# An RWKV-5 and mixture-of-experts kernel: the loads of an item's r and k, and of its keys and values, cut in two

## The chip, the cores and the metric

The kernel runs on one core of one Trainium2 chip. The metric is the device time of one execution in microseconds (us). The kernel before took 382.85 us, the median of three runs (382.5 to 382.89).

## The reference, cut to what matters

An attention block of the RWKV-5 kind is followed by a mixture of experts that routes each token to one expert. Batch B = 4, heads H = 8, sequence S = 768, head dimension 48; all values are float32.

```python
for t in range(S):                                   # attention, for each batch and head
    cur = einsum('bhd,bhe->bhde', u * k[t], v[t])
    y[t] = einsum('bhd,bhde->bhe', r[t], state + cur)
    state = w * state + einsum('bhd,bhe->bhde', k[t], v[t])
x = y as (B, S, 384)
for b, s:                                            # mixture of experts
    fresh = argmax(x[b, s] @ w_gate)                 # 8 experts
    e = fresh, or the token's before it where sigmoid(x[b, s] @ w_local) >= 0.5
    out[b, s] = softmax(x[b, s] @ w_gate)[e] * (relu(x[b, s] @ w1[e]) @ w2[e])   # 384 -> 1024 -> 384
```

## The kernel before, in words

The attention is computed in 16 items. An item is one batch and one pair of heads (`n` from 0 to 15, `b, hp = divmod(n, 4)`), with the sequence cut into NCH = 6 chunks of 128 tokens. For an item TensorE computes the scores of a chunk against itself (`scores`, L288), the part of a token's own key (`own`, L267), the keys times values that a chunk adds to the state (`added`, L248), and the outputs from inside the chunk (`inside`, L297) and from the states before it (`before`, L310). VectorE masks the scores (L290), multiplies by v (L273), scans over the states (L254) and divides the keys by the decay (`keys`, L236). GpSimd prepares three products for each item (`scale`): `pd`, r times k (L216); `rw`, r times the decay (L229, for the first three items on VectorE); `ke`, the keys of the states times the decay (L212). ScalarE copies the outputs from PSUM (L318, and L331 after they are turned), and when a batch of four items is done it stores the batch with one transfer to memory, `x_d` (L334).

An item's input comes by `load(n)`, called three items ahead in `run`. Three DRAM arrays are read, each with 128 partition rows for an item:

- `rk`, 768 KB: a row has the 768 values of r and then the 768 values of k, 6144 bytes. Four tiles take turns (`AHEAD` = 4).
- `kv`, 584 KB: a row has the 576 values of the keys (`VB` = 576) and then the 592 of the values with their padding, 4672 bytes. Five tiles take turns. `ke` (L212) reads the keys and `added` and `inside` read the values.
- `vT`, 384 KB: v turned, 3072 bytes in a row, read by L273. Four tiles take turns.

All these transfers are issued by SyncE (SP), which does nothing else here and issues in the order of the program. It waits before each transfer until the tile that it overwrites is free. It also waits for one of eight semaphores: the builder puts the transfers of SP and ScalarE into one order and gives them the eight in turn, so each waits until the transfer eight places before it in that order has landed. The same holds for ScalarE's `x_d`: the wait stands in ScalarE's own queue, and the copies of later items stand behind it.

Item 0 is a case of its own: its `rk` already comes by two transfers, one for chunks 0 to 2 and one for chunks 3 to 5.

The order of the work on each engine is the order in which `run` calls the steps; no scheduler reorders it. After the 16 items the experts follow: ten blocks of tokens (`Experts.run`), with a block's weights `w1t` and `w2t` loaded by SP and ScalarE, tokens gathered from `x_d` and results scattered to the output by GpSimd.

Of the kernel before, what the change touches and what calls it, by code (L numbers as in the profile page):

```python
# [21 lines left out]
B, H, S, DH = 4, 8, 768, 48  # L22
# [30 lines left out]
VB = NCH * 2 * DH  # L53
# [8 lines left out]
class Attention:  # L62
# [126 lines left out]
    def load(self, n):  # L189
        nc = self.nc  # L190
        b, hp = divmod(n, HP)
        rk, vT, kv = self.rks[n % AHEAD], self.vTs[n % AHEAD], self.kvs[n % (AHEAD + 1)]
        if n:
            nc.sync.dma_start(out=rk.rearrange("p a c t -> p (a c t)"), in_=self.rk_d[b, hp])
        else:
            for z in (slice(0, C2), slice(C2, NCH)):
                nc.sync.dma_start(out=rk[:, :, z], in_=self.rk_d[b, hp].rearrange("p (a c t) -> p a c t", a=2, c=NCH)[:, :, z])
        nc.sync.dma_start(out=kv, in_=self.kv_d[b, hp])
        nc.sync.dma_start(out=vT.rearrange("p a c t -> p (a c t)"), in_=self.vT_d[b, hp])
        self.items[n].update(b=b, hp=hp, rT=rk[:, 0], kT=rk[:, 1], vT=vT,  # L200
                             k=kv[:, :VB].rearrange("p (c x) -> p c x", c=NCH), v=kv[:, VB:])
# [1549 lines left out]
```

## Time and profile before

| | before |
|---|---|
| median of three runs | 382.85 us (382.5 to 382.89) |
| the profiled execution | 382.2 us |
| its span, first to last instruction | 380.4 us |
| TensorE clock granted, share of full | 0.997 |
| PE busy | 366.9 us, 96% |
| DVE busy | 248.7 us, 65% |
| POOL busy | 151.3 us, 40% |
| ACT busy | 107.1 us, 28% |
| DMA | 17765 packets, 74.97 MB |
| rk, time from issue to landing | 5.7 / 9.0 / 12.2 us (least, median, most) |
| kv, time from issue to landing | 6.1 / 7.7 / 12.6 us |

The profile is of one execution. The page gives busy times of each engine, 40 slices of the span (9.5 us each), the DMA queues and the costliest groups of instructions. PE is TensorE's matmuls and PEld its weight loads. A busy PE isn't PE at its peak, since the ends of pipelined matmuls are modelled. A line that ends in `[1.51 <-DMA kv<-in_kv_dram]` says that the engine was idle for 1.51 us and that the landing of that transfer ended the idle time. `ACTq` and `SPq` are the sequencers, which issue transfers while the engine itself is idle.

The loads of the items run from 0.8 to about 85 us, the attention to about 110 us.

### The profile page before, as it was taken

What the parts mean: (1) busy time and instruction counts of PE and PEld (TensorE: products, weight loads), DVE (VectorE), ACT (ScalarE), POOL (GpSimd) and SP (SyncE); (2) the same over time, 40 slices, a digit from 0 to 9 for tenths busy, and PEclk for the clock granted to TensorE, in tenths of its full rate; (3) what the DMA queues carried; (4) which work ended last, traced back from release to release, by engine and by line L of the source; (5) the groups of instructions that cost most, each with busy time, mean ns of one, the idle gap of its engine ahead of it and who ended that gap; (6) DMA issues with size and microseconds to landing.
All of it is one profiled execution on the core that took longest, in us unless ns stands there. A gap on an engine that the chain in (4) does not pass through costs nothing. (4 is left out here: it accounts for less than half of the span.)

```text
span 380.4 us, 9693 instructions
## 1 busy us (share of the span) xinstructions
PE 366.9 (96%) x3846; PEld 323.9 (85%) x3846; DVE 248.7 (65%) x720; ACT 107.1 (28%) x295; POOL 151.3 (40%) x213
## 2 busy tenths in 40 slices
PE   8999999999999999999999999999999999999992
PEld 7776777776769989999999999999898899899971
DVE  6888778887853736587557857758658758466400
ACT  4132233232322112223323233233233233232210
POOL 8789999886222043211423213223323123012022
PEclk9999999999999999999999999999999999999998
DMA  7999999973648872811561254146146156063011
GB/s 254 412 411 407 408 398 310 372 307 126 210 157 301 318 274 68 317 60 40 200 219 41 72 209 179 38 173 227 57 167 229 37 179 229 12 225 161 3 37 36
DMA packets 17765, 74.97 MB, mean 197 GB/s; under 512 B 2761, under 2 KB 6618, under 8 KB 15408
## 3 DMA queue, kind: packets, MB, share of 16 engines
q1 hardware_dynamic: 10336, 56.89, 40.1%
q0 software_dynamic: 3424, 9.52, 7.6%
q10 hardware_dynamic: 3952, 7.87, 5.7%
q8 instruction: 32, 0.52, 0.6%
q14 instruction: 21, 0.17, 0.1%
HBM read 64.83 MB, written 9.51 MB: 195 GB/s over the span
## 5 line engine op out<-in xcount | busy, mean ns | idle before, releaser
L1308 POOL DMA_INDIRECT out_dram<-yo,sid x27 | 26.6, 987 | 102.4 <-ACT yo L1303 79.0
L1159 PE MATMUL h<-exT,w1t 128*128 128x168 f32 (+4 forms) x240 | 54.9, 327 | 0.0
L1163 DVE TENSOR_TENSOR hT<-h,hs 128x168 f32<-128x168 f32 (+3 forms) x60 | 21.1, 351 | 46.3 <-PE h L1159 30.5
L1082 POOL DMA_INDIRECT xg<-x_d,gid x29 | 31.1, 1074 | 35.7 <-DVE sm L905 17.4
L1159 PEld LDWEIGHTS h<-exT,w1t 128*128 128x128 f32 x240 | 41.7, 190 | 0.3 <-issue 0.3
L1109 PE MATMUL h<-exT,w1t 128*128 128x192 f32 (+1 forms) x192 | 38.3, 338 | 0.0
L1228 PE MATMUL y<-factors,sums 128*128 128x192 f32 x168 | 36.8, 326 | 0.0
L1159 PE MATMUL h<-xs,ws 128*128 128x168 f32 (+4 forms) x144 | 35.2, 326 | 0.0
L216 POOL TENSOR_TENSOR pd<-rk 128x384 f32<-128x384 f32 x32 | 31.4, 1002 | 8.6 <-PE y L267 6.2
L290 DVE TENSOR_TENSOR am<-pair,kept 128x768 f32<-128x768 f32 x32 | 30.0, 951 | 7.1 <-PE pair L288 6.9
L1109 PEld LDWEIGHTS h<-exT,w1t 128*128 128x128 f32 x192 | 32.3, 190 | 1.5 <-issue 0.2
L1159 PEld LDWEIGHTS h<-xs,ws 128*128 128x128 f32 x144 | 25.5, 190 | 4.3 <-ACT hs L1166 1.2
L1228 PEld LDWEIGHTS y<-factors,sums 128*128 128x128 f32 x168 | 28.9, 190 | 0.0
L212 POOL TENSOR_TENSOR ke<-kv,endT 128x288 f32<-128x288 f32 x32 | 24.9, 799 | 1.8 <-DMA kv<-in_kv_dram 1.8
L288 PE MATMUL pair<-rw,kw 48*64 48x128 f32 (+1 forms) x768 | 23.5, 249 | 1.3 <-DVE lt L349 0.4
L297 PE MATMUL y<-am,kv 128*64 128x128 f32 x360 | 23.9, 276 | 0.8 <-DVE y L273 0.8
L229 POOL TENSOR_TENSOR rw<-rk,tab 128x384 f32<-128x384 f32 x26 | 23.6, 929 | 0.2 <-DMA rk<-in_rk_dram 0.2
L1228 PE MATMUL y<-w2t,hT 128*128 128x192 f32 x96 | 23.0, 328 | 0.0
L1096 DVE COPY exT<-tp 128x384 f32<-128x384 f32 (+6 forms) x29 | 14.0, 489 | 13.7 <-PE tp L1095 13.5
L288 PEld LDWEIGHTS pair<-rw,kw 48*64 48x64 f32 x768 | 19.6, 133 | 3.8 <-issue 2.1
L297 PEld LDWEIGHTS y<-am,kv 128*64 128x64 f32 x360 | 20.0, 137 | 2.4 <-DVE y L273 1.0
L318 ACT COPY xT<-y 128x768 f32<-128x768 f32 x15 | 12.0, 799 | 34.0 <-PE y L310 34.0
(301 smaller groups left out, 737.9 us busy)
## 6 DMA issues: line engine op xcount, KB each, us to landing
w1t<-in_w_dram SPq DMA_DIRECT2D x8, 1536.0 KB, 6.7
w2t<-in_w_dram SPq DMA_DIRECT2D x8, 1536.0 KB, 7.2
rk<-in_rk_dram SPq DMA_DIRECT2D x15, 768.0 KB, 9.0
kv<-in_kv_dram SPq DMA_DIRECT2D x16, 584.0 KB, 7.7
vT<-in_vT_dram SPq DMA_DIRECT2D x16, 384.0 KB, 8.3
x_d<-x ACTq DMA_DIRECT2D x4, 1152.0 KB, 4.6
w1t<-in_w_dram SPq DMA_DIRECT2D x2, 768.0 KB
w2t<-in_w_dram SPq DMA_DIRECT2D x2, 768.0 KB, 4.5
```

The lines of the kernel that those rows point to most:

```text
L212: nc.gpsimd.tensor_mul(t["ke"][:, p::2], t["k"][:, p::2], spread(self.endT[:, p, hp], 1, C2))
L216: nc.gpsimd.tensor_mul(t["pd"][:, z], t["rT"][:, z], t["kT"][:, z])
L229: engine.tensor_mul(t["rw"][:, z], t["rT"][:, z], spread(pw, 1, z.stop - z.start))
L288: nc.tensor.matmul(sc[f * DP:(f + 1) * DP, h, i, x:], lhsT=t["kw"][q, c, o * DP:(o + 1) * DP], rhs=t["rw"][q, c, x:], start=True, stop=True)
L290: return lambda: nc.vector.tensor_mul(t["am"][:, g], sc, spread(self.kept[:, g:g + 3], 1, 2))
L297: nc.tensor.matmul(t["y"][h][p * DP:(p + 1) * DP, c2 * P:(c2 + 1) * P], lhsT=t["v"][:, (2 * c + h) * DH:(2 * c + h) * DH + DP], rhs=t["am" ...
L1082: self.nc.gpsimd.indirect_dma_start(out=xg[:n], out_offset=None, in_=self.x_d[:rows], in_offset=bass.IndirectOffsetOnAxis(ap=u["gid"][:n, ...
L1109: nc.tensor.matmul(h[:, :n], lhsT=u["w1"][:, m, kk, :], rhs=u["xT"][:, kk, :], start=(kk == 0), stop=(kk == DK - 1))
L1159: nc.tensor.matmul(out, lhsT=a, rhs=b, start=start and k == 0, stop=stop and k == len(terms) - 1, skip_group_check=True)
L1163: nc.vector.tensor_tensor(out, a, b, op=Alu.add)
L1228: return lambda: nc.tensor.matmul(bank[:, x * half:(x + 1) * half], lhsT=a, rhs=b, start=(j == 0 and x == 0), stop=(j == FK // 2 - 1), ski ...
L1308: self.nc.gpsimd.indirect_dma_start(out=out.rearrange("n (h d) -> (n h) d", h=2) if half else out, out_offset=bass.IndirectOffsetOnAxis(ap ...
```

## The change

`load` issues `rk` (for items 1 to 15) and `kv` (for all items) as two transfers instead of one. The r half and the k half of `rk` have rows of 3072 bytes; the keys' half of `kv` has rows of 2304 bytes and the values' half of 2368. The same bytes go to the same places of the same tiles. Who waits for a tile now waits for the half that it reads. `vT`, item 0's `rk` and everything else in the source stay.

```diff
         if n:
-            nc.sync.dma_start(out=rk.rearrange("p a c t -> p (a c t)"), in_=self.rk_d[b, hp])
+            for a in range(2):
+                nc.sync.dma_start(out=rk[:, a].rearrange("p c t -> p (c t)"), in_=self.rk_d[b, hp][:, a * S:(a + 1) * S])
         else:
             for z in (slice(0, C2), slice(C2, NCH)):
                 nc.sync.dma_start(out=rk[:, :, z], in_=self.rk_d[b, hp].rearrange("p (a c t) -> p a c t", a=2, c=NCH)[:, :, z])
-        nc.sync.dma_start(out=kv, in_=self.kv_d[b, hp])
+        for z in (slice(0, VB), slice(VB, None)):
+            nc.sync.dma_start(out=kv[:, z], in_=self.kv_d[b, hp][:, z])
         nc.sync.dma_start(out=vT.rearrange("p a c t -> p (a c t)"), in_=self.vT_d[b, hp])
```

## The prediction

> **What bounds the kernel now.** I read the page first, for where PE is full and where the transfers are.
>
> ```profile
> span 380.4 us, 9693 instructions
> ...
> PE   8999999999999999999999999999999999999992
> ...
> POOL 8789999886222043211423213223323123012022
> ...
> DMA  7999999973648872811561254146146156063011
> GB/s 254 412 411 407 408 398 310 372 307 126 210 157 301 318 274 68 317 60 40 200 219 41 72 209 179 38 173 227 57 167 229 37 179 229 12 225 161 3 37 36
> ```
>
> A digit is a tenth of a slice of 9.5 us. PE is full from the second slice to the end. The transfers are full only in the slices up to about 60 us, at some 410 GB/s, while the items' inputs come in. The chain that ended last says nothing here (it breaks off after 1 us, at the last scatter), so I asked the list of waits for the first 110 us, where all of the change lies.
>
> ```profile
> POOL pd L216 <- DMA rk<-in_rk_dram: 2.4, 2, 1.3
> ...
> POOL ke L212 <- DMA kv<-in_kv_dram: 1.8, 2, 1.5
> ...
> PEld mp L248 <- POOL ke L212: 1.2, 2, 0.6
> ```
>
> The columns are us in total, times, and longest. GpSimd is the only engine that waits for these loads, 4.4 us with one wait of 0.2 for rw, all in the first 28 us. TensorE never waits for one. The list for PE alone has 1.5 us of GpSimd, for the identity at the start, and after that only VectorE (0.9, 0.8, 0.5, 0.4) and small rests. The 1.2 us above is of weight loads (PEld), which run ahead of the matmuls; PE itself had no gap there. So the question is how far GpSimd is ahead of PE when it waits. The timelines of the two, GpSimd first:
>
> ```profile
> 11.15 1.96 POOL L216 TENSOR_TENSOR pd<-rk 128x384 f32<-128x384 f32 x2 [1.04 <-DMA rk<-in_rk_dram]
> ...
> 27.50 1.55 POOL L212 TENSOR_TENSOR ke<-kv,endT 128x288 f32<-128x288 f32 x2 [1.51 <-DMA kv<-in_kv_dram]
> ```
>
> ```profile
> 15.45 0.90 PE L267 MATMUL y<-pd,w_t 48*64 48x384 f32 x8
> ...
> 30.24 0.65 PE L248 MATMUL mp<-kv,ke 128*48 128x48 f32 x20
> ```
>
> Item 1's pd ends at 13.1 and is used at 15.45. Item 4's ke ends at 29.05 and is used at 30.24, behind PE's own work without a gap. The margins are 2.3 and 1.2 us, and the second is the smallest I find. Items 2 and 3 have 3 us or more. Followed back from 47 us, PE's order goes through VectorE, one ScalarE copy and itself, and reaches no transfer and no GpSimd work but the identity at 1.5 us. From 44 us on PE has next to no gap, so whatever delays it before that arrives whole at the end.
>
> The last view is ScalarE's timeline around the first store of x_d, and PE's after it.
>
> ```profile
> 40.77 0.40 ACTq L334 DMA_DIRECT2D x_d<-x  x1
> 43.82 0.80 ACT L318 COPY xT<-y 128x768 f32<-128x768 f32 x1 [3.09 <-PE y L310]
> ```
>
> ```profile
> 44.68 0.88 PE L267 MATMUL y<-pd,w_t 48*64 48x384 f32 x8
> ```
>
> The copy ends at 44.62 and frees the only buffer of y; PE's L267 starts at 44.68. This copy is on the path that sets the end, and the store of x_d stands ahead of it in ScalarE's queue.
>
> **What the Trainium skill says.** The page "DMA: Bandwidth & Descriptors" has three sections that bear on this. "Why small descriptors are slow (HBM only)" puts a fixed cost on each packet. The trace agrees: its packets on SP's queue take 234 ns (median) with 6144 bytes, 180 with 4672, 121 with 3072 and 65 with 1536, which is a line of 0.0366 ns a byte plus 9 ns. "Why a DMA increments its semaphore by 16 and not by 1" says that a transfer has landed only when all its engines have counted. The trace agrees: item 8's rk counts first at 40.40 and last at 43.12. "Queues, rings and completion order" says that an engine takes its rows in turn, a packet at a time. The store of x_d, landing 13.4 us after its issue amid a full SP queue, fits that.
>
> **The change part by part.**
>
> *Packets.* A transfer of 128 rows gives each of 16 engines 8 packets and one count of 9 ns. One rk was 8 x 234 + 9 and becomes 2 x (8 x 121 + 9): 73 ns more. One kv was 8 x 180 + 9; halves of 2304 and 2368 bytes are 93.3 and 95.7 ns on the line: 8 x 9 + 9, some 80 ns more. An item had 4.31 us of packets and gets 4.46. That is 0.15 us more an item (3.5%). Up to item 8 it adds 1.2 us to a landing, over all 16 items 2.4 us. It is hidden: item 1's rk lands at 11.23 instead of 11.08 and pd ends at 13.3, used at 15.45. Later items land ahead of use, rk 5 to 11 (issued 18.65 to 52.68, landed 30.21, 34.49, 38.77, 43.12, 48.23, 54.40, 58.66; first used by rw at 32.85 to 64.18) by 2.6 to 5.5 us, more than the 0.75 to 1.7 us added. Without that cover it would be up to 2.4 us.
>
> *Issue.* 31 more transfers at 0.33 us each (up to 0.6 at the start) are 10 us or so on SP over 80 us. SP waits there anyway: 26.9 us for VectorE's y alone. Nothing computes on SP.
>
> *Finer waits.* rw needs only r, kw only k, ke only the keys. Item 4's keys land 0.1 to 0.9 us earlier (half a kv is 0.73 us at 410 GB/s, less 0.64 us of extra packets, and the slowest engine's lag falls on one half or the other). GpSimd's wait of 1.51 us becomes 0.6 to 1.4. pd needs both halves, so its two waits grow by 0.15 and 0.3 us. PE takes nothing of it, by the margins above: worth 0. GpSimd gets an extra semaphore wait for many pd, at 17 to 51 ns for such an instruction, 16 of them under 0.8 us, on an engine that is ahead.
>
> *Eight semaphores in turn.* Eight transfers were 2.7 items and are now 1.6, some 2.8 MB, 6.9 us of work at 410 GB/s. A load in this stage lands 10 to 12 us after its issue because it queues; now about 7. The engines don't run dry: the slowest lags the fastest by up to 2.7 us, and a piece of weights issued onto idle engines counts after 3.6 us of which 1.9 are its own packets. That leaves 6.9 - 0.9 - 2.7 = 3.3 us of work against 1.7 of delay. Cost 0.
>
> *The store of x_d.* This is the part that can show. By the listing of the changed program the first store (0.40 us on ScalarE) now takes the semaphore of **item 8's r half**; before it was that of item 6's vT, landed at 36.88, long before 40.77. When does the r half land? Before, item 8's rk landed at 43.12. Add 1.2 us of packets and take off the k half, 8 x 121 + 9 = 0.98: 43.34. The store then ends at about 43.8, and L318 behind it was to start at 43.82. Behind L318 waits L267 and all of PE. So the central cost is 0 with no margin: each 0.1 us of lateness costs 0.1 us. The trace has no such halves with a stride of twice their length, so I bound it. From below, with the packets' overhead overlapped, the half lands at 42.2 and costs 0; a gain through it is excluded, since the copy waits for PE anyway. From above, the mean of vT's packets while the loads run is 132 ns instead of 121; with 2 x 132 against a mean of 249, and the same on kv, the overhead is some 0.26 us an item, 2.1 us by item 8, and the half lands at 44.2, costing 0.85 us. I take 0.15 us. The other three stores find their semaphores free: by the listing they follow loads of items 11, 14 and 15, landed at about 60, 79 and 84 us against stores at 64.64, 90.25 and 114.89. The first store's later landing (about 53 us) holds up item 11's r, which has 5.5 us to spare.
>
> *Sum.* 0 + 0 + 0 + 0.15. The profiled execution would go from 382.2 to about 382.35 (span 380.4 to 380.55). It lay 0.65 us under the median of the runs; on the median it is 382.85 + 0.15 = 383.0 us.
>
> **The rivals.**
>
> *The store stops ScalarE.* Slower, by one mechanism: item 8's r half lands later than about 43.35 us, L334 waits for it, L318 behind it, L267 behind that. For it: no margin in the sum. Against: the landing comes out just at the limit. At the upper bound it costs 0.85 us, 383.7 us; a further instruction-fetch packet on the slowest engine (16 KB, 1.0 us median in this trace) makes it 384.6. It counts as slower from a landing at about 44.1.
>
> *GpSimd's waits were on the path.* For it: 4.4 us of waits for these loads, and GpSimd full from 28 to 67 us. If half a kv were saved there and PE followed, 0.7 to 1.4 us: 381.5 to 382.1 us. Against: margins of 1.2 us and more, and GpSimd waits for PE at 69, 81 and 94 us.
>
> *The loads pace the stage.* Then the 0.15 us an item count, 16 x 0.15 = 2.4 us: 385.2 us. Against: PE has no wait for a load, and the loads end at 85 us, the items at 110.
>
> *The change does nothing at all.* 382.85 us; it can't be told from my forecast.
>
> **How the numbers follow.** Forecast (with no effect) 0.58, 382.5 to 383.5 around 383.0. ScalarE stopped by more than the bound 0.23, GpSimd's waits on the path 0.14, loads as the pace 0.05. A measurement of this kernel can't tell 0.2%, 0.77 us, from no change. Faster than 382.08: most of the third case, 0.12. Slower than 383.62: the second and fourth, 0.28. Same: 0.60, the forecast with what is small of the others. The range has the forecast, the second up to its 0.85 us and somewhat over, and the weak end of the third: 382.1 to 384.1.
>
> **What would show it.** Right: rk and kv land 7 us after issue; SP's packets grow by 31 x 144 = 4464; an item's loads pace at 4.46 us; GpSimd's wait for kv shrinks and those for rk grow a little, with PE's times up to 43 us within 0.1; L334's first store at 43.3 to 43.4 instead of 40.77. Wrong: L318 of item 4 starts later than 43.9 (second case), PE reaches 43 us earlier (third), or PE or PEld wait for a load (fourth).

## The result, and the profile after

| | before | after |
|---|---|---|
| median, on one chip | 382.6 us (381.78 to 385.73) | 383.45 us (382.29 to 387.21) |
| the profiled execution | 382.2 us | 382.74 us |
| its span | 380.4 us | 381.0 us |
| packets of SP's queue | 10336 | 14800 |
| rk, median from issue to landing | 9.0 us | 6.7 us |
| kv, the same | 7.7 us | 7.2 us (keys), 6.3 us (values) |

The ratio is 1.0031, with a 95% interval of 1.0015 to 1.0046; the medians themselves differ by 0.85 us. A second comparison, on chip 3, gave 1.0044 (1.0028 to 1.0061), and 1.54 us between the medians. By the ratios the change makes the kernel about 0.3 to 0.4% slower, 1.2 to 1.7 us. Here and below the medians are of all executions, and the ratios leave out those more than 1.5% above the fastest of their kernel, which matters for `odd_even`, `merged`, `by_partitions` and `used_rows`.

From the page of the changed kernel, the rows that answer to those shown of before:

```profile
span 381.0 us, 9728 instructions
...
PE   7999999999999999999999999999999999999992
...
DMA  7999999993657871820661254146146156064011
GB/s 256 400 397 397 396 391 350 361 319 131 192 175 272 326 293 52 313 79 22 218 215 45 62 207 186 43 173 221 63 167 227 39 179 229 10 225 163 3 37 36
```

The second to sixth slice carried 412 to 398 GB/s before and carry 400 to 391 now. That is 3% less, what the packets' fixed cost takes. The engines are as full as before (row DMA), so the backlog of loads lasts longer.

The waits of the first 110 us in the changed kernel (us in total, times, longest):

```profile
POOL pd L218 <- DMA rk<-in_rk_dram: 2.3, 2, 1.6
PEld mp L250 <- POOL ke L214: 1.8, 3, 0.6
...
POOL ke L214 <- DMA kv<-in_kv_dram: 0.6, 1, 0.6
```

GpSimd's wait for kv went from 1.8 to 0.6 us and that for rk from 2.4 to 2.3. In the list of PE's own waits still no line names a transfer. GpSimd's timeline shows the same two instructions as before, and then PE's:

```profile
11.23 1.96 POOL L218 TENSOR_TENSOR pd<-rk 128x384 f32<-128x384 f32 x2 [0.67 <-DMA rk<-in_rk_dram]
...
26.34 1.56 POOL L214 TENSOR_TENSOR ke<-kv,endT 128x288 f32<-128x288 f32 x2 [0.56 <-DMA kv<-in_kv_dram]
```

```profile
15.91 0.90 PE L269 MATMUL y<-pd,w_t 48*64 48x384 f32 x8
...
30.70 0.66 PE L250 MATMUL mp<-kv,ke 128*48 128x48 f32 x20
```

Item 4's `ke` starts at 26.34 instead of 27.50, but PE uses it at 30.70 instead of 30.24. GpSimd gained over a microsecond and PE took none of it. PE's 0.46 us of delay in this execution come from its start: `w_t`, a transfer that the change doesn't touch, landed at 3.26 us instead of 2.81. In most other kernels below it landed at 2.76 to 2.83, so this delay is of one execution. ScalarE around the first store, and PE after it:

```profile
42.61 0.40 ACTq L336 DMA_DIRECT2D x_d<-x  x1
44.23 0.80 ACT L320 COPY xT<-y 128x768 f32<-128x768 f32 x1 [3.23 <-PE y L312]
```

```profile
45.08 0.88 PE L269 MATMUL y<-pd,w_t 48*64 48x384 f32 x8
```

The store did wait for item 8's r half, which landed at 42.53. But it was issued 1.6 us before the copy behind it could start, and the copy waited for PE alone.

So where is the time? I compared the start of each PE matmul with the same matmul of the kernel before. In a second profiled execution of the change (`after_again`, span 381.7) PE is 0.33 us ahead at 45 us, 1.14 us behind at 66 us, and 1.30 us behind at the end of the program. The loss arises between 46 and 66 us. PE's timeline there shows it, first before and then `after_again`:

```profile
51.80 0.71 PE L248 MATMUL mp<-kv,ke 128*48 128x48 f32 x20
57.09 0.66 PE L248 MATMUL mp<-kv,ke 128*48 128x48 f32 x20
```

```profile
51.47 0.29 PE L250 MATMUL mp<-kv,ke 128*48 128x48 f32 x3
52.16 0.57 PE L250 MATMUL mp<-kv,ke 128*48 128x48 f32 x17 [0.40 <-issue]
...
57.31 0.29 PE L250 MATMUL mp<-kv,ke 128*48 128x48 f32 x4
57.98 0.56 PE L250 MATMUL mp<-kv,ke 128*48 128x48 f32 x16 [0.38 <-issue]
```

Twenty matmuls of one kind, with the same inputs, break off after the third or fourth. "issue" means that PE waited for nothing that the profile shows. These two breaks cost 0.55 and 0.54 us, and a third at 63.4 us 0.38. That is the whole 1.47 us. The first profiled execution, the one of the table above, shows less of it: PE ends 0.63 us behind, of which `w_t` accounts for 0.45, and of these three breaks it has only the first, with 0.27 us. How many breaks there are differs from one execution to the next.

The breaks stand at fixed places of PE's program. Counted from its start these are among matmuls 725, 852, 978, 1105, 1231, and on in steps of 126 or 127. The table of queues has a row for such a rhythm:

```profile
q8 instruction: 32, 0.52, 0.5%
```

These are 32 packets of 16 KB with PE's instructions, about 1 us each. The Trainium skill, "Runtime: NRT & Kernel Launch", section "Instruction fetch mechanics", says that a sequencer fetches its program through a DMA queue of its own in blocks of 16 KiB, which are 256 instructions. The trace agrees on the size: 127 matmuls with a weight load each are 254. I call such a block a page, and its first matmul its boundary. The same section calls the crossing of a block mostly hidden. Here it isn't. From the packets' times in the traces, for the pages that begin at five of these matmuls: how long after the previous page's boundary the fetch started, how long after the fetch's end PE ran the page's first matmul (both us), and the largest distance between the starts of two matmuls there (ns; about 100 at most where nothing stops PE there).

```
matmul          725              852              978              1105             1231
before        3.78 1.46 392   3.70 1.44 323   2.99 1.38  73   1.11 2.39  38   1.61 2.46   7
after         3.97 1.51 538   3.70 1.44 328   3.14 1.52 330   1.68 2.22  39   2.19 1.89   7
after_again   3.79 1.39 264   3.73 1.40 326   3.56 1.33 606   3.35 1.41 585   3.14 1.35 316
extra_packets 3.70 1.49 265   3.58 1.56 327   3.67 1.52 880   3.33 1.42 600   3.32 1.09 316
fewer_bytes   3.89 1.55 540   1.12 3.21  74   2.31 2.02  73   2.64 1.69  38   0.60 3.65   7
```

(The last two kernels are explained below.) PE never runs a page sooner than 1.09 us after its fetch has ended. Where its distance is 230 ns or more, that lag is always 1.1 to 1.6 us; this holds over the pages from 725 to 1991 in all the traces, apart from matmul 1864, where PE waits for VectorE, and from `by_partitions`, where PE waits for data too. With the engines full of loads the fetch starts 3.0 to 4.0 us after the boundary; with room on them, often at 1 to 2 us. In the first case a page takes 3.7 + 1.0 + 1.45 = 6.2 us. PE runs a page in 5.3 us or so here (before, 51.94 to 57.22). So PE is paced by its own instructions while the load queue is full. Before, that held for pages 725 and 852 and just not for 978. (Outside the table it also held for pages 600 and 1612, with distances of 363 and 452 ns, 1.43 and 1.45 us after a fetch's end.) After, of the pages from 978 to 1231 one stops PE in `after` and all three in `after_again`. I call this the fetch theory. The 0.33 us by which `after_again` leads at 45 us have the same source: pages 600 and 725 stopped it 0.19 and 0.13 us less than before.

### The profile page after: what moved, and what is told of

Same layout as the page of the kernel before. It is cut to its first block, busy times and chain, and to the rows that moved or that the text cites. A ratio compares the mean times of both kernels' runs of the same rounds, so it can differ in the third digit from the quotient of the medians.

```text
span 381.0 us, 9728 instructions
## 1 busy us (share of the span) xinstructions
PE 367.0 (96%) x3846; PEld 323.8 (85%) x3846; DVE 248.2 (65%) x720; ACT 107.1 (28%) x295; POOL 151.2 (40%) x213
## 3 DMA queue, kind: packets, MB, share of 16 engines
q1 hardware_dynamic: 14800, 56.89, 40.6%
## 5 line engine op out<-in xcount | busy, mean ns | idle before, releaser
L299 PE MATMUL y<-am,kv 128*64 128x128 f32 x360 | 23.9, 276 | 0.8 <-DVE y L275 0.8
L299 PEld LDWEIGHTS y<-am,kv 128*64 128x64 f32 x360 | 20.0, 137 | 2.4 <-DVE y L275 1.0
```

The costliest lines, as they stand in the source:

```text
L299: nc.tensor.matmul(t["y"][h][p * DP:(p + 1) * DP, c2 * P:(c2 + 1) * P], lhsT=t["v"][:, (2 * c + h) * DH:(2 * c + h) * DH + DP], rhs=t["am" ...
```

## The experiments

Each ratio is to the kernel before on the same chip, with a 95% interval. Differences are to the changed kernel where nothing else is said.

### The change again, each half of it, and the store moved

These four were compared together, before the fetch theory was formed. The change itself:

> The changed kernel once more, beside the others on one chip, as their yardstick. The store theory (ScalarE's first store of x_d waits for item 8's r half, and the copy L320 behind it starts late when that half lands after about 43.8 us) and the packet theory (0.15 us more of packets an item delays work somewhere) both expect +0.2 to +0.3% against the kernel before; the store theory also expects single runs that scatter upward by 1 us and more. If the difference was an accident of the first measurement, it is within 0.1%.

Measured: 383.95 us, ratio 1.0044 (1.0028 to 1.0061). Its trace is the one shown above.

`rk_only` cuts rk and leaves kv whole; `kv_only` the reverse.

```diff
 rk_only
-        for z in (slice(0, VB), slice(VB, None)):
-            nc.sync.dma_start(out=kv[:, z], in_=self.kv_d[b, hp][:, z])
+        nc.sync.dma_start(out=kv, in_=self.kv_d[b, hp])
 kv_only
-            for a in range(2):
-                nc.sync.dma_start(out=rk[:, a].rearrange("p c t -> p (c t)"), in_=self.rk_d[b, hp][:, a * S:(a + 1) * S])
+            nc.sync.dma_start(out=rk.rearrange("p a c t -> p (a c t)"), in_=self.rk_d[b, hp])
```

> Only rk by two transfers. The first store's semaphore is then that of item 7's kv, expected to land at about 40.8 us, well before the copy behind it is due. The store theory expects no loss: within 0.1% of the kernel before. The packet theory expects about half: +0.1 to +0.15%.

> Only kv by two transfers. The first store's semaphore is that of the values' half of item 7, expected to land at about 40.9 us, before the copy behind it is due. The store theory expects no loss: within 0.1%. The packet theory expects about half: +0.1 to +0.15%. If finer waits for the keys help GpSimd and through it PE, this one is faster than before.

Measured: `rk_only` 382.89 us, ratio 1.0015 (1.0001 to 1.0029); `kv_only` 382.78 us, ratio 1.0012 (1.0003 to 1.0021). Each half costs something, and together they come to 1.0027, within the interval of the whole. No single half, and no wait for a single half, is the cause. It is something that adds up.

`late_store` issues the store of `x_d` behind the copy that stood behind it (`turn` keeps the tile in `self.unsent`, and `store()` sends it after `before`).

```diff
 turn
-            nc.scalar.dma_start(out=self.x_d[...], in_=x)
+            self.unsent = b, x
 run
             self.before(n - 1)
+            self.store()
```

> The changed kernel with the stores of x_d moved in ScalarE's order behind the copy L320 of the same round, so that their wait for a semaphore has nothing urgent behind it. The store theory expects the loss to go: within 0.1% of the kernel before. The packet theory expects it to stay: +0.2 to +0.3%. In the profile L320 of item 4 starts within 0.05 us of PE's end in both cases.

Measured: 383.6 us, ratio 1.0038 (1.0026 to 1.005). ScalarE in `late_store`, the store now behind the copy:

```profile
43.52 0.80 ACT L321 COPY xT<-y 128x768 f32<-128x768 f32 x1 [3.02 <-PE y L313]
43.72 0.40 ACTq L344 DMA_DIRECT2D x_d<-x  x1
```

The store can stop nothing there, and the loss stays. The store theory falls.

### Packet time without a cut: `extra_packets`

The kernel before, and one small transfer more an item.

```diff
+        self.extra = once.tile([P, 8, 64], F32, name="extra")
 load (of the kernel before, rk and kv whole)
         nc.sync.dma_start(out=vT.rearrange("p a c t -> p (a c t)"), in_=self.vT_d[b, hp])
+        nc.sync.dma_start(out=self.extra[:, n % 8], in_=self.rk_d[b, hp][:, :64])
```

> The kernel before, with rk, kv and vT whole, and after each vT one more transfer of 128 rows of 256 bytes into a tile that nobody reads: 8 x (9 + 9.4) + 9 = 156 ns of packets an item, about what the change adds (153), without cutting anything. Packet and fetch theory: as slow as the change, ratio 1.0015 to 1.0045, GB/s of the stretch 3% lower on data (some 400), PE's gaps at its instruction pages in more places than before. Rival, the cut of rk and kv itself (finer waits, five transfers an item): 0.9995 to 1.001.

Measured: 383.56 us against 381.77, ratio 1.0045 (1.003 to 1.006). The packets of 256 bytes took 18 ns each. PE at the same two places:

```profile
51.40 0.29 PE L250 MATMUL mp<-kv,ke 128*48 128x48 f32 x3
52.36 0.57 PE L250 MATMUL mp<-kv,ke 128*48 128x48 f32 x17 [0.67 <-issue]
...
57.52 0.29 PE L250 MATMUL mp<-kv,ke 128*48 128x48 f32 x4
58.21 0.56 PE L250 MATMUL mp<-kv,ke 128*48 128x48 f32 x16 [0.39 <-issue]
```

The change's loss is there with no load cut: the same packet time, the same places, the same size. The rival that the cut itself costs (finer waits, five transfers an item) expected at most 1.001, and falls. It does add a fourth transfer to an item's three, so the number of transfers could still be what costs. The two runs above speak against that. `rk_only` and `kv_only` also have four transfers an item (item 0's `rk` apart) and as many packets more as this kernel, but they add 73 and 80 ns of packet time an item instead of 156, and they cost 0.15 and 0.12% instead of 0.45%. The intervals don't meet (at most 1.0029 against at least 1.003), though they were taken on two chips. The loss follows the packets' time and not their number.

This trace, the slowest of the kernel's seven executions, also lost 1.66 us at a later page (matmul 1612, fetch 5.64 us after the boundary), and the break had a second cost. Two matmuls lie 2.11 us apart there; from 84.62 us on the granted clock was 0.50 for 3.41 us, and in that stretch PE lost another 1.45 us. The traces of before, `after` and `after_again` have no such stretch between 7 and 377 us, so it is no part of the loss shown above. The whole loss at the end of this trace is thus more than its median shows.

### The loads made shorter: `fewer_bytes`

```diff
-        nc.sync.dma_start(out=vT.rearrange("p a c t -> p (a c t)"), in_=self.vT_d[b, hp])
+        if n not in range(4, 11):
+            nc.sync.dma_start(out=vT.rearrange("p a c t -> p (a c t)"), in_=self.vT_d[b, hp])
```

> The change, but vT of items 4 to 10 isn't loaded, so their y is multiplied by an older item's v: this leaves out 2.75 MB of loads and no computation. Every half of rk and kv is as in the change. Fetch theory: with 1.0 us less of packets an item the engines aren't full from about 45 us on, instruction fetches start 1 to 2 us after the page before instead of 3 to 4, PE's gaps at 52, 58 and 63 us go, ratio 0.996 to 1.0005. Rivals in which the halves themselves cost (their waits on GpSimd, number of transfers, the store of x_d): the loss of the change stays, 1.003 to 1.0045.

The total, 2767.3 us, answers nothing: with other values of x the routing went to the program's general path for the experts, which is another program. The attention ran as in the change, and its PE timeline can be read:

```profile
51.44 0.66 PE L251 MATMUL mp<-kv,ke 128*48 128x48 f32 x20
56.73 0.66 PE L251 MATMUL mp<-kv,ke 128*48 128x48 f32 x20
```

Both breaks are gone, as the table's last row says, though every half of rk and kv is loaded as in the change. At matmul 1612 PE is 0.80 us ahead of the kernel before (79.00 against 79.80), where `after_again` is 1.1 us behind (80.92). The expectation in the ratio stays untested; that on the places was met, and the fetches of pages 852 to 1231 started 0.6 to 2.6 us after the boundary where 1 to 2 were expected.

### The pages moved in PE's program: `shifted`

```diff
-        self.align(26)
+        self.align(0)
```

> The change without the 26 small matmuls of `align` at the start (they compute nothing that is used). PE's program is 26 matmuls shorter ahead of the attention, so that the pages in which PE's instructions come (126 to 127 matmuls each) end 26 matmuls later in the program. Fetch theory: the gaps of PE without a releaser near 40, 52 and 58 us leave L250 (at its 3rd to 5th matmul of 20) and turn up 26 matmuls later, in L299 after its 8th to 10th matmul of 24, whichever of these pages is late in this execution; they stand again 1.3 to 1.5 us after the end of the page's fetch. Rival, something that L250 itself waits for and the trace doesn't show (ke, the buffer mp): the gaps stay at L250. Time: 1.001 to 1.006 of before, since the fetches come as late as before.

The 26 calls are 52 matmuls in the trace (3846 before, 3794 here), so the places had to move by 52, not 26. Counted from the fourth matmul of L250, 52 further are 17 of L250, 24 of L299 and 11 of L312. PE in `shifted`:

```profile
47.41 0.65 PE L250 MATMUL mp<-kv,ke 128*48 128x48 f32 x20
...
49.36 0.68 PE L312 MATMUL y<-rw,S 48*48 48x128 f32 x11
50.28 0.56 PE L312 MATMUL y<-rw,S 48*48 48x128 f32 x9 [0.25 <-issue]
...
55.22 0.68 PE L312 MATMUL y<-rw,S 48*48 48x128 f32 x11
56.08 0.48 PE L312 MATMUL y<-rw,S 48*48 48x128 f32 x9 [0.18 <-issue]
...
60.96 0.68 PE L312 MATMUL y<-rw,S 48*48 48x128 f32 x12
63.01 0.48 PE L312 MATMUL y<-rw,S 48*48 48x128 f32 x8 [1.37 <-issue]
```

The breaks left L250, which runs whole, and stand in L312 after its 11th or 12th matmul, 1.40, 1.32 and 1.40 us after the end of a fetch. Against `after_again`, matmul by matmul, PE gains 0.26, 0.32, 0.60 and 0.55 us at the four old places and loses 0.51, 0.45 and 1.55 at the three new ones shown. Nothing that L250 waits for is the cause; the page is. The time, 387.62 us, ratio 1.0138 (1.0104 to 1.0172), missed the expected 1.001 to 1.006. By 12 us 1.76 us were lost, before any of this. The trace's first record of the full clock stands at 11.39 us instead of 6.37, and until then PE ran slower (five matmuls of L163 took 1.27 us against 0.71), which fits that the matmuls left out, though nothing reads what they compute, have a use. And the pages happened to collide worse (1.55 us at 63 us, 1.10 at 81).

### More of the same: `vT_too`

```diff
-        nc.sync.dma_start(out=vT.rearrange("p a c t -> p (a c t)"), in_=self.vT_d[b, hp])
+        for a in range(2):
+            nc.sync.dma_start(out=vT[:, a].rearrange("p c t -> p (c t)"), in_=self.vT_d[b, hp][:, a * C2 * P:(a + 1) * C2 * P])
```

> The change, and vT also by two transfers with rows of 1536 bytes: another 8 x 9 + 9 = 81 ns of packets an item on top of the 153 of the change. Fetch theory: half as much loss again or more, ratio 1.0045 to 1.008, GB/s in the slices up to 60 us about 390 instead of 397, and PE's gaps without a releaser at its instruction pages in one or two more places. If the loss of the change came only from who waits for which half of rk and kv, nothing is added: 1.003 to 1.0045.

Measured: 384.89 us, ratio 1.0059 (1.0038 to 1.0081), with 394 to 375 GB/s in the slices. The size is as expected, the mechanism is not. With these shorter packets pages 725 and 852 were fetched 2.8 and 3.0 us after the boundary and stopped nothing; PE was 1.2 us ahead of before at 39 us. Then came the wait that my prediction had feared for the change. ScalarE in `vT_too`, and PE behind it:

```profile
44.29 0.40 ACTq L337 DMA_DIRECT2D x_d<-x  x1
44.73 0.80 ACT L321 COPY xT<-y 128x768 f32<-128x768 f32 x1 [4.77 <-DMA rk<-in_rk_dram]
```

```profile
45.58 0.99 PE L270 MATMUL y<-pd,w_t 48*64 48x384 f32 x8 [2.00 <-ACT xT L321]
```

Here the store takes the semaphore of item 8's k half, which landed at 44.21. The copy waits for it, and PE stands for 2.00 us. The fetch of page 1738 came 5.8 us after the boundary and cost another 2.4 us in this execution, the slowest of ten. After each of these two breaks the granted clock was 0.50 for 3.41 us (from 46.21 and from 90.59 us). That shorter packets brought the fetches of 725 and 852 earlier, with more packet time in all, the fetch theory does not explain.

### As many transfers, packets of full length: `by_partitions` and `odd_even`

Both cut rk and kv by rows instead of along them: `by_partitions` into rows 0 to 63 and 64 to 127, `odd_even` into even and odd rows. Shown are the new lines for rk; those for kv are alike.

```diff
 by_partitions
+            for q in (slice(0, DP), slice(DP, P)):
+                nc.sync.dma_start(out=rk[q].rearrange("p a c t -> p (a c t)"), in_=self.rk_d[b, hp][q])
 odd_even
+            for o in range(2):
+                nc.sync.dma_start(out=rk.rearrange("(q o) a c t -> o q (a c t)", o=2)[o], in_=self.rk_d[b, hp].rearrange("(q o) x -> o q x", o=2)[o])
```

> rk (items 1 to 15) and kv are each cut in two by partitions, 64 rows of full length each: as many transfers and semaphores as in the change, but the packets of the kernel before. Fetch theory (longer packet work keeps the engines full for longer, and PE then waits for its own instructions, which come over the same engines): packets as before but for two more counts of 9 ns an item, so at most 0.02 us an item; ratio 0.9995 to 1.001, PE's gaps at its instruction pages as in the kernel before. Rival, number of transfers (the eight semaphores then cover 1.6 items instead of 2.7): as slow as the change, ratio 1.003 to 1.0045.

Measured: 425.04 us, ratio 1.1068 (1.102 to 1.1117). From its page:

```profile
GB/s 201 232 233 230 228 248 207 245 226 208 237 233 274 283 85 303 349 146 210 186 21 186 202 40 136 221 58 159 212 51 167 219 20 227 147 144 203 3 33 32
...
L231 POOL TENSOR_TENSOR rw<-rk,tab 128x384 f32<-128x384 f32 x26 | 23.5, 927 | 28.8 <-DMA rk<-in_rk_dram 28.8
```

The loads ran at 230 GB/s, a packet of 6144 bytes took 447 ns (median up to 57 us) instead of 235, and then the loads do pace the stage: GpSimd waits 28.8 us for them. I should have known this ahead. The Trainium skill, "SBUF — State Buffer", section "Door 1: The DMA port swizzle", says that partitions 0 to 63 reach only 8 of 16 ports, with half the bandwidth. The trace agrees.

> rk (items 1 to 15) and kv are each cut in two by even and odd rows, 64 rows of full length each: as many transfers, semaphores and waits as in the change, with the packets of the kernel before but two more counts of 9 ns an item. The cut into lower and upper rows ran at half the rate (230 GB/s), since a transfer then wrote to half of the partitions at a time; these rows lie over all partitions. If it runs at the full 410 GB/s: packet theory 0.9995 to 1.0012; rival, number of transfers and waits: 1.003 to 1.0045. If it runs at half the rate too, it is slower by 5 to 10% and tells nothing on the question.

Measured: 386.52 us, ratio 1.0086 (1.0056 to 1.0116). These rows ran at the full rate, 408 GB/s from 9 to 28 us. But the kernel doesn't answer the question. SP issued no load from 34.6 to 45.88 us, went on when the store of `x_d` had landed (45.81), and the engines meanwhile fell to half their load (172 GB/s from 38 to 48 us). In that pause the pages 852 and 978 were fetched 0.69 and 0.22 us after their boundaries, and PE was 1.03 us ahead of before at 45.6. Later, with the loads behind, PE lost more than that.

### Two tries for a faster kernel: `used_rows` and `merged`

If loads delay PE's instructions, less to load should help. `used_rows` leaves out the rows of padding of rk and vT (16 of each 64) from item 4 on, in two transfers of 48 rows. Shown are the new lines.

```diff
 load (of the kernel before)
+        rows = (slice(0, P),) if n < AHEAD else (slice(0, DH), slice(DP, DP + DH))
+            for q in rows:
+                nc.sync.dma_start(out=rk[q].rearrange("p a c t -> p (a c t)"), in_=self.rk_d[b, hp][q])
+        for q in rows:
+            nc.sync.dma_start(out=vT[q].rearrange("p a c t -> p (a c t)"), in_=self.vT_d[b, hp][q])
```

> The kernel before, but from item 4 on only the rows of rk and vT that hold data are loaded (48 of each 64), as two transfers of 48 rows of full length each; the rows of padding keep what an earlier item left there. Five transfers an item as in the change, packets 3.6 us an item instead of 4.3 (14 fewer... 6 of rk and 6 of vT instead of 8 and 8, with kv unchanged). Fetch theory: the full stretch ends some microseconds earlier, PE's gaps at the instruction pages after about 45 us go, ratio 0.996 to 0.9987. Rival, number of transfers: slower than before, 1.001 to 1.0045. Rival, the loads don't matter to PE at all: 1.000.

Measured: 403.52 us, ratio 1.0508 (1.0473 to 1.0544). It failed for the reason of `by_partitions`: 211 to 253 GB/s in the slices in which these transfers run. There the fetches took their turn later still: PE had distances of 1.6 to 2.7 us at pages 978, 1358, 1485 and 1738, each 1.40 to 1.46 us after a fetch had ended.

`merged` puts vT behind r and k in one array and one tile, so that from item 5 on one transfer with rows of 9216 bytes brings all three. Shown are the new lines of `load`.

```diff
 load (of the kernel before)
+        if n > 4:
+            nc.sync.dma_start(out=rk.rearrange("p a c t -> p (a c t)"), in_=self.rk_d[b, hp])   # tile [P, 3, NCH, P]
+        if n < 5:
+            nc.sync.dma_start(out=vT.rearrange("p a c t -> p (a c t)"), in_=self.rk_d[b, hp][:, 2 * S:])
```

> The mirror of the change: rk and vT lie in one DRAM array and one tile, and from item 5 on come by one transfer with rows of 9216 bytes: 81 ns of packets an item less, 0.9 us over 11 items. Packet and fetch theory: the stretch ends up to 0.9 us earlier, ratio 0.9975 to 1.0002. Rival, transfers finer is better (rk now lands together with vT, 1 us later): 1.000 to 1.003.

Measured: 387.88 us, ratio 1.0132 (1.0082 to 1.0182), a miss for both. Its trace lost most at the start, where nothing was merged yet. VectorE in `merged`:

```profile
4.70 0.17 DVE L124 TENSOR_SCALAR w<-w_t 128x4 f32<-128x4 f32 x1 [2.74 <-DMA w_t<-in_wu_dram]
```

`w_t` is issued at the same 0.82 us as item 0's rk and landed at 4.68 instead of 2.81, behind it. PE's matmuls that need what follows from it came 1.87 us later than before, and after that pause the granted clock was 0.50 from 9.61 to 13.02 us, which made it 3.36 us. PE was 2.9 us behind before at 37 us. From there to matmul 1612 it lost nothing more (2.6 us behind): the joint tile comes free later, the loads ran at 300 to 318 GB/s from 28 to 57 us, and of the pages up to 1231 only 852 stopped PE (a distance of 0.33 us). That fits the fetch theory, but the median lies further above before than this trace does. What the rest is stays open, and no version here beats the kernel before.

## Why the prediction was right or wrong

The time fell into the range, and that was luck: the cause was wrong and the effect larger than forecast. I forecast 383.0 us in 382.1 to 384.1; it came to 383.45. But of these 383.0 the change was to make up 0.15 us, all by the store, and it cost 0.85 us between the medians, 1.2 us by the ratio, and nothing by the store. The kernel before came out at 382.6 us with more executions, under the 382.85 that I had started from, which hid part of the miss. I gave "same" 0.60, up to 383.62 us. The median lies within it, but the ratio shows that the kernel is slower.

- **Packets.** Their number is exact (4464 more), and so is their cost: 3% less GB/s, and 256-byte packets at 18 ns where the line gives 18.4. The failed step is "It is hidden". I checked the cover of the items' data, and it held: no wait of PE for a load shows in these traces. I didn't ask who else is served by those engines. PE's instructions are, and they had no cover: before, page 978 was ready 1.38 us ahead, at the limit. The step's own price "up to 2.4 us" without cover was the right scale: 1.7 us by `extra_packets`.
- **Issue.** Right at 0: SP issued 31 transfers more and no wait for it shows, though its issuing of the items' loads grew from 21.6 to 37.4 us, more than the 10 us or so of the forecast.
- **Finer waits.** Right at 0 for PE, in spite of more than a microsecond gained on GpSimd. The wait for item 4's keys, 0.56 us, lies just under the forecast 0.6 to 1.4. The two waits for rk were to grow by 0.15 and 0.3 us. In `after_again` they went from 1.04 and 1.34 to 1.23 and 1.75, by 0.19 and 0.41, near the forecast. In `after` GpSimd itself came late, and the first fell to 0.67.
- **Eight semaphores in turn.** Right: rk and kv land 6.3 to 7.2 us after issue and the engines stay full.
- **The store of x_d.** The wait is there, but the r half landed at 42.53, not 43.34, near my lower bound of 42.2. The term that was off is item 8's landing before, 43.12: it held some 0.8 us by which one slow engine lagged in that execution. The cost was 0 and not 0.15, as `late_store` confirms. The mechanism is real, as `vT_too` shows with 2.00 us.
- **PE's times up to 43 us** were to agree within 0.1. They don't: 0.40 us late in one execution of the change (`w_t`), 0.33 early in the other (pages 600 and 725).
- **The rivals.** "The store stops ScalarE" is excluded. So is GpSimd's wait on the path. "The loads pace the stage" had named packet time as what PE pays for, which is right, but by PE's wait for a load, which isn't there. My store rival named an instruction-fetch packet only as 1.0 us of work in front of a load. I had the packet in view and looked at the wrong one of the two that wait.

What stays open: why a fetch starts 3 to 4 us after the boundary when the queue is full, when a load packet of 6144 bytes takes 0.235 us. It also scatters between executions and at later pages (up to 5.8 us), which fits the wide spread of times of one kernel; that it causes the spread was not shown. The clock has a part in it: the slowest execution in each comparison of the change, 387.21 and 387.73 us, had a mean granted clock of 0.989 and 0.985, where most had 0.993 to 0.997. The places of the breaks rest on one trace of the kernel before and two of the change, with the other kernels' beside them.

## What to carry to other kernels

A full DMA stretch has a customer that no list of tiles names: the instructions of a busy engine. Where PE runs many short matmuls under full loads, look for breaks in a group of like matmuls with no releaser, at equal counts of instructions, and set the fetch packets' ends beside them. Packet time added there is not free even when every tile lands early. And look at the granted clock behind a long break: in `extra_packets` a break that cost 1.66 us cost another 1.45 that way.

## What the runs showed of the hardware that was not expected

- PE's instructions come in pages of 126 to 127 matmuls with their weight loads. PE ran a page no sooner than 1.09 us after its 1 us packet ended. With loads at about 400 GB/s a page took 6.2 us, and PE uses one in 5.3.
- 64 rows in one half of the partitions load at 230 GB/s; 64 even or odd rows at 408.
- A small transfer issued together with a large one at the start landed at 2.76 to 3.26 us in all kernels but one, and at 4.68 in that one; PE started that much later (0.45 us with 3.26, 1.87 with 4.68).
- After some breaks of PE the granted clock fell to 0.50 for 3.41 us. In `extra_packets`, `vT_too` (twice) and `merged` this began 0.6 to 1.8 us after the end of a break of 1.8 to 2.6 us, and cost 1.2 to 1.6 us more. In `odd_even` it followed one break of 1.74 us and not one of 1.73; in `shifted` one of 1.64 us had none behind it.
